# Splitting the last loads of a layer into quarters, in an attention-and-MLP decode kernel on one core

## The chip, the cores and the metric

The kernel runs on one core of one Trainium2 chip. The metric is the device time of one execution in microseconds (us). "Before" is the tuned kernel, "after" is the same kernel with the change. The runs quoted here are of the state "fast".

Names used below: TensorE (PE in the profile, PEld its weight loads), VectorE (DVE), ScalarE (ACT), the sync engine's queue (SPq), which issues all loads, and the 16 DMA engines, which move them.

## The reference, cut to what matters

Two layers of the same thing: attention of one query per batch entry and head over a cached K and V, a projection with `wo`, and an MLP with `w3` and `w4`.

```python
B, Sq, D = 2, 1, 576
H, Sk, Dh = 32, 16384, 128          # K and V: 4 MB each for one (batch, head), bf16
# ...
    q = (x @ wq) ...
    scores = einsum("bhqd,bhkd->bhqk", q, k_cache) * (Dh ** -0.5)
    o = einsum("bhqk,bhkd->bhqd", softmax(scores), v_cache)
    return o... @ wo
# ...
    h2 = gelu(layernorm(x1) @ w3) @ w4
# x -> attention -> MLP -> attention -> MLP, the same weights and caches in both layers
```

There are 64 units (batch x head), each with 8 MB of K and V. They are read in both layers, except for two units that stay on the chip from layer 1 to layer 2. That makes about 1.1 GB of loads with very little arithmetic for each byte.

## The kernel before

One large buffer has three places of 8 MB, each for the K and V of one unit. Weights are laid over parts of the places that are free at the time. `want` queues a load; `pump` issues loads strictly in order, and holds the first one (and with it all behind it) until everything that lies under its destination has been used.

```python
    def pump(self):
        while self.queue:
            keys, p, n, src, sem = self.queue[0]
            under = [t for t in self.live if t["off"] < p + n and p < t["off"] + t["n"]]
            if not all(t["done"] for t in under):
                return
            # ... waits for the readers of what lies under it, then one DMA for each src
```

K and V of a unit come whole (4 MB each), but those of the last unit of a layer, and the first that layer 2 loads, come in halves of 2 MB:

```python
            if split:
                ap = src.rearrange("(t p j) d -> t p (j d)", t=2, p=128)
                for h in range(2):
                    ring.want([(kind, l, u, h)], at + h * self.half, self.half,
                              [lambda e, v, h=h: e.dma_start(v, ap[h])])
            # ...
        for i in range(U - 3, U):                      # the last three V of a layer
            kv("V", l, i, split=i == U - 1)
        want_w34(l, 1, 1 if l == 0 else 2)             # behind them w3 and w4
        if l == 0:
            want_wq(1, 1)                              # and layer 2's wq
```

The second half of the last V lies over the last piece of `wo` (three heads), which is used in the middle of the last unit:

```python
                if i == U - 1 and c == 3:              # last unit, after its fourth chunk
                    self.weigh(l, i - 2, 0)
                    self.weigh(l, i - 2, 1)
                    self.normalize(*mid, self.o[:, slice(*mid)], "o")
                    self.project_pieces(l, [self.n_wo - 1])     # uses wo's last piece
```

So the order at the end of a layer is: all loads up to the first half of the last V are queued some 30 us ahead; then the queue waits for the projection; then come the second half, `w3` and `w4`. `W4_PIECES = (5, 4, 2, 1)` says in how many feature groups `w4` comes; the first piece has a place of its own, the second lies over `w3` in layer 1 and waits until the first two rows of `w3` are used. `weigh` multiplies with a V half only when it has landed:

```python
        vt, res = self.ring.get(self.key("V", l, u, h))
        # ... 64 matmuls with vt
        self.pe(f, r=[*res, f"p{q}"], w=[f"P:ops{q}"])
```

TensorE's instructions of the middle units stand in a loop (two units a turn), those of the other engines are unrolled:

```python
                def run(eng, items=plan[e], loops=self.loops if e == "tensor" else ()):
```

Of the kernel before, what the change touches and what calls it, by code (L numbers as in the profile page):

```python
# [189 lines left out]
class Arena:  # L190
# [34 lines left out]
    def get(self, key):  # L225
        t = self.tiles[key]
        return self.buf[:, t["off"]:t["off"] + t["n"]], t["res"]
# [6 lines left out]
class Decode:  # L234
# [5 lines left out]
    ROT = 12  # L240
    WO_PIECE = 4
    FJ = 3
    W4_PIECES = (5, 4, 2, 1)

    def __init__(self, nc, A_x, K, V, wq, wo, w2, w3, w4, out):
        self.nc = nc
# [91 lines left out]
    def plan(self):  # L338
        ring, B, H, D, KT, U = self.ring, self.B, self.H, self.D, self.KT, self.U
        unit = 2 * self.half  # L340
        self.order = [list(range(U)), list(reversed(range(U)))]
        self.kept = set(self.order[0][-self.N_KEEP:])

        def kv(kind, l, i, split=False):
            u = self.order[l][i]
            if l == 1 and u in self.kept:
                return
            b, hh = u % B, u // B
            src = {"K": self.K, "V": self.V}[kind][b, hh]
            pl = self.place(l, i)  # L350
            at = pl * self.place_n + {"K": 0, "V": unit}[kind]
            if split:
                ap = src.rearrange("(t p j) d -> t p (j d)", t=2, p=128)
                for h in range(2):
                    ring.want([(kind, l, u, h)], at + h * self.half, self.half,
                              [lambda e, v, h=h: e.dma_start(v, ap[h])])
            else:
                ap = src.rearrange("(p j) d -> p (j d)", p=128)
                ring.want([(kind, l, u, h) for h in range(2)], at, unit, [lambda e, v: e.dma_start(v, ap)],
                          sem=f"{kind}{pl}")  # L360

        def rows(kind, l, w, at, last=None):


            n = w.shape[1]
            for k in range(KT):
                if k < KT - 1:
                    ap, m = w[k * 128:(k + 1) * 128, :], n
                else:
                    m = n // 2  # L370
                    ap = w[k * 128:D, :].rearrange("r (c n) -> (r c) n", c=2)
                ring.want([(kind, l, k)], at + k * n if last is None or k < KT - 1 else last, m,
                          [lambda e, v, ap=ap: e.dma_start(v, ap)])  # L373

        def want_wq(l, p):
            rows("wq", l, self.wq, p * self.place_n + unit, last=p * self.place_n + 7 * unit // 8)

        def want_w34(l, p, p1):
            base = p * self.place_n
            rows("w3", l, self.w3, base)  # L380
            at, a0 = base + (2 * KT - 1) * self.F // 2, 0
            for c, n in enumerate(self.W4_PIECES):
                m = n * self.FJ * D
                if c == 1:
                    assert at <= base + self.place_n
                    at = p1 * self.place_n
                ap = self.w4[a0 * 128 * self.FJ:(a0 + n) * 128 * self.FJ, :].rearrange(
                    "(a p j) n -> p a (j n)", p=128, j=self.FJ)
                ring.want([("w4", l, c)], at, m,
                          [lambda e, v, ap=ap, n=n: e.dma_start(v.rearrange("p (a m) -> p a m", a=n), ap)])  # L390
                at, a0 = at + m, a0 + n

        def want_w2(at):
            n = 128 * (KT - 1)
            w2a, w2b = self.w2[0:n, :].rearrange("(p r) n -> p (r n)", p=128), self.w2[n:D, :]
            ring.want([("w2",)], at, KT * D, [lambda e, v: e.dma_start(v[:, 0:(KT - 1) * D], w2a),
                                              lambda e, v: e.dma_start(v[0:64, (KT - 1) * D:KT * D], w2b)])

        def want_wo(l, j, at):
            h0, h1 = self.wo_piece(l, j)  # L400
            ap = self.wo[h0 * 128:h1 * 128, :].rearrange("(j p) n -> p j n", p=128)
            ring.want([("wo", l, j)], at, (h1 - h0) * D,
                      [lambda e, v: e.dma_start(v.rearrange("p (j n) -> p j n", n=D), ap)])

        want_wq(0, 2)
        for l in range(2):
            wp = 2 - 2 * l
            early = 5 if l == 1 else 0
            wo_at = 7 if l == 0 else self.ROT + 1
            gap = max(1, (U - 8 - wo_at) // self.n_wo)  # L410
            for i in range(U):
                kv("K", l, i, split=(l == 1 and i == 2) or i == U - 1)
                if i < early:
                    kv("V", l, i, split=(l == 1 and i == 2))
                elif early <= i - 1 < U - 3:
                    kv("V", l, i - 1)
                j, r = divmod(i - wo_at, gap)
                if r == 0 and 0 <= j < self.n_wo:
                    want_wo(l, j, wp * self.place_n + (2 * unit - self.N_MID * D if j == self.n_wo - 1
                                                            else j * self.WO_PIECE * D))  # L420
                if l == 0 and i == 6:
                    want_w2(wp * self.place_n + unit)
            for i in range(U - 3, U):
                kv("V", l, i, split=i == U - 1)
            want_w34(l, 1, 1 if l == 0 else 2)
            if l == 0:
                want_wq(1, 1)
# [7 lines left out]
        ap = self.wo[h * 128:(h + 1) * 128, :]  # L435
        self.s.dma(lambda e: e.dma_start(self.wolast[:, :], ap), w=["wolast"])

    def key(self, kind, l, u, h):
        return (kind, 0 if u in self.kept else l, u, h)

    def release(self, kind, l, u, h):
        if l == 1 or u not in self.kept:
            self.ring.done(self.key(kind, l, u, h))


    def build(self):
# [215 lines left out]
    def turn(self, l, i, c):  # L662

        u = self.order[l][i]
        h, j0 = divmod(c * self.CH, self.TB)
        kt, res = self.ring.get(self.key("K", l, u, h))
        b, k = c % 3, c % self.NKT

        def f(pe):
            for j in range(self.CH):  # L670
                ins = pe.transpose(self.tps[b][:, j * 128:(j + 1) * 128],  # L671
                                   kt[:, (j0 + j) * 128:(j0 + j + 1) * 128], self.ident[:, :])
            return ins
        self.pe(f, r=[*res, "ident"], w=[f"P:tps{b}"])
        self.act(lambda a: a.activation(out=self.ktsb[k][:, :, :].rearrange("p a b -> p (a b)"), in_=self.tps[b][:, :],  # L675
                                        func=ACT.Copy), r=[f"P:tps{b}"], w=[f"ktsb{k}"])
        self.waiting.append((l, i, c, k))
        if (c + 1) * self.CH == self.TB:
            self.release("K", l, u, 0)
# [13 lines left out]
    def dots(self, l, i, c):  # L693
        u = self.order[l][i]
        h, j0 = divmod(c * self.CH, self.TB)
        kt, res = self.ring.get(self.key("K", l, u, h))
        d = c % 2
        q = i % 2
        k3 = kt.rearrange("p (j d) -> p j d", d=128)[:, j0:j0 + self.CH, :]
        self.dve(lambda v: v.tensor_tensor(out=self.prod[d][:, :, :], in0=k3, in1=bcast_mid(self.qb[q][:, :], self.CH),  # L700
                                           op=ALU.mult), r=[*res, f"qb{q}"], w=[f"prod{d}"])
        o = c * self.CH - self.NCP * self.CH
        self.dve(lambda v: v.tensor_reduce(out=self.sd[q][:, o:o + self.CH], in_=self.prod[d][:, :, :], axis=AX.X,  # L703
                                           op=ALU.add), r=[f"prod{d}"], w=[f"sd{q}"])
        if (c + 1) * self.CH == self.NB:
            self.release("K", l, u, 1)
# [30 lines left out]
    def weigh(self, l, i, h):  # L737
        u = self.order[l][i]
        q = i % 2
        vt, res = self.ring.get(self.key("V", l, u, h))  # L740

        def f(pe):
            for j in range(self.TB):
                ins = pe.matmul(self.ops[q][:, 0:1], lhsT=vt[:, j * 128:(j + 1) * 128],  # L744
                                rhs=self.p[q][:, h * self.TB + j:h * self.TB + j + 1],
                                start=(h == 0 and j == 0), stop=(h == 1 and j == self.TB - 1))
            return ins
        self.pe(f, r=[*res, f"p{q}"], w=[f"P:ops{q}"])
        self.release("V", l, u, h)
        if h == 1 and i < self.U - 1:  # L750
            self.dve(lambda v: v.tensor_copy(out=self.o[:, u:u + 1], in_=self.ops[q][:, 0:1]),
                     r=[f"P:ops{q}"], w=["o"])
# [150 lines left out]
```

## Time and profile before

| | before |
|---|---|
| median of 3 runs | 2578.07 us (2577.87 to 2578.26) |
| loads | 1099.39 MB, mean 427 GB/s |
| DMA busy | 9 tenths or more in 39 of 40 slices |
| busy share of VectorE, TensorE, ScalarE | 77%, 60%, 43% |

The lines of the page of before that bound the kernel: the span; the 40 slices of DMA share and GB/s; and the DMA queues with packets, MB and share of the 16 engines' time.

```profile
span 2575.9 us, 75345 instructions
...
DMA  9999999999999999999999999999999999999998
GB/s 414 431 427 432 431 432 430 432 429 430 433 432 431 431 432 431 432 430 428 406 401 427 428 430 430 430 431 432 431 432 430 430 432 431 431 431 432 429 427 357
...
q1 hardware_dynamic: 51944, 1097.76, 99.6%
q8 instruction: 80, 1.31, 0.2%
q14 instruction: 39, 0.32, 0.0%
```

The loads fill the span. GB/s falls in slices 20 and 21 (end of layer 1, start of layer 2) and in the last one: there, if anywhere, a reordering of loads can gain. The table of stretches of before shows those dips more finely. Its columns: the stretch in us, busy time (and count) of PE, PEld, DVE, ACT, POOL, then the granted TensorE clock, the DMA share and GB/s.

```profile
1266.00:1268.00 2.00, 1.32 (x50) 1.23 (x47) 1.97 (x3) 0.00 (x0) 0.00 (x0) 0.50 0.71 303
1268.00:1270.00 2.00, 0.15 (x5) 0.15 (x6) 1.73 (x4) 0.00 (x0) 0.00 (x0) 0.50 0.68 279
1270.00:1272.00 2.00, 2.00 (x38) 2.00 (x37) 1.51 (x3) 0.67 (x1) 0.00 (x0) 0.50 0.84 229
1272.00:1274.00 2.00, 2.00 (x34) 2.00 (x32) 1.97 (x3) 2.00 (x7) 0.00 (x0) 0.50 0.75 295
...
1294.00:1296.00 2.00, 2.00 (x78) 2.00 (x76) 0.00 (x0) 0.00 (x0) 0.00 (x0) 0.50 0.87 297
1296.00:1298.00 2.00, 1.10 (x40) 1.01 (x37) 0.28 (x2) 0.49 (x2) 0.00 (x0) 0.50 0.85 304
...
2530.00:2532.00 2.00, 1.47 (x55) 1.38 (x52) 1.97 (x3) 0.00 (x0) 0.00 (x0) 0.50 0.82 352
2532.00:2534.00 2.00, 0.00 (x0) 0.00 (x1) 1.88 (x4) 0.00 (x0) 0.00 (x0) 0.50 0.49 197
2534.00:2536.00 2.00, 2.00 (x37) 2.00 (x38) 1.37 (x3) 0.53 (x1) 0.00 (x0) 0.50 0.76 279
2536.00:2538.00 2.00, 2.00 (x33) 2.00 (x32) 1.97 (x3) 2.00 (x7) 0.00 (x0) 0.50 0.93 393
```

Against 430 GB/s the stretches from 1266 to 1274 lose 2.9 us of stream and those from 2530 to 2538 lose 2.3 us (each loses 2 us times what it lacks of 430, over 430). The wait behind the second dip, in the sync queue's own list of waits (line, who ended it, us in total, times, longest):

```profile
SPq L356 <- PE misc L581: 30.2, 1, 30.2
```

Line 356 is the issue of the second half, line 581 is the projection with `wo`. Last, the tail of the chain of waits of before (start, us, what):

```profile
2556.91 15.06 DMA buf<-in_B_w_dram
2571.98 0.05 issue
2572.03 0.57 PE misc L581 x15
```

The kernel ends with a fixed tail of 3.9 us behind the landing of `w4`'s last piece at 2571.98. Whatever is to speed up the end has to bring that landing forward.

The Trainium skill, page "DMA: Bandwidth & Descriptors", section "Why a DMA increments its semaphore by 16 and not by 1", says that the engines of a load finish independently, each adds one to the load's semaphore, and only the full count means that everything has landed. The trace file has the time of every one of these 16 increments (they were read from the file itself; no view of the profile prints them), so it shows not only when a load was complete, but how far apart its fastest and its slowest engine were. They are not told by name; the table gives the first, the 15th and the last. End of layer 2 in before (us from the span's start):

```
load                    issued    first    15th     last
last V, first half      2503.93   2531.04  2539.83  2541.95
last V, second half     2534.59   2541.24  2545.65  2546.85
w3, first rows          2534.96   2543.99  2548.43  2549.63
w4, last piece          2556.91   2566.40  2571.12  2571.98
```

Between the two halves the first increments lie 10.20 us apart, although 2 MB take 4.88 us: the fastest engine stood dry for 5.3 us, that is, it had no load queued. The last ones lie 4.90 us apart: the slowest did not stand at all. This takes it that one and the same engine is last both times. The trace does not name it, but an engine that is done with the first half at 2541.95 and needs 4.88 us for its share of the second cannot be done before 2546.83, and the last increment came at 2546.85.

### The profile page before, as it was taken

How to read it: one execution, taken by the hardware profiler on the slowest of the kernel's cores; microseconds unless marked ns; L12 is line 12 of the kernel's file. 1: busy time of each engine (PE TensorE's matmuls, PEld its weight loads, DVE VectorE, ACT ScalarE, POOL GpSimd, SP SyncE). 2: the span in 40 equal slices, each digit the busy share in tenths (PEclk: the TensorE clock that was granted, in tenths of full speed). 3: DMA queues.
4: the chain of work that ended last, by engine and by line, in shares of the span. 5: the costliest groups of instructions: out<-in, count | busy, mean ns of one | idle time of the engine just before them, and what ended most of it. 6: DMA issues, size and time to landing. Idle time of an engine off the chain costs nothing.

```text
span 2575.9 us, 75345 instructions
## 1 busy us (share of the span) xinstructions
PE 1546.1 (60%) x34519; PEld 1459.3 (57%) x34519; DVE 1977.9 (77%) x2781; ACT 1111.2 (43%) x1809; POOL 0.8 (0%) x10
## 2 busy tenths in 40 slices
PE   5655555655556555656667765556555555566666
PEld 5555555555555555555657765555555555555555
DVE  5877787778777777878759987777787777778875
ACT  3444444444444444444435544444444444444442
POOL 0000000000000000000000000000000000000000
PEclk8666666666666666666655666666666666666665
DMA  9999999999999999999999999999999999999998
GB/s 414 431 427 432 431 432 430 432 429 430 433 432 431 431 432 431 432 430 428 406 401 427 428 430 430 430 431 432 431 432 430 430 432 431 431 431 432 429 427 357
DMA packets 52063, 1099.39 MB, mean 427 GB/s; under 512 B 4900, under 2 KB 13160, under 8 KB 16872
## 3 DMA queue, kind: packets, MB, share of 16 engines
q1 hardware_dynamic: 51944, 1097.76, 99.6%
q8 instruction: 80, 1.31, 0.2%
q14 instruction: 39, 0.32, 0.0%
HBM read 1097.74 MB, written 0.00 MB: 426 GB/s over the span
## 4 chain that ended last, share of the span: by engine, by line
DMA 54%; DVE 38%; PE 6%; SPq 1%; issue 1%; ACT 0%; DVEq 0%
DMA buf<-in_A_k_cache_dram 52%; DVE sd L703 24%; DVE prod L700 13%; PE tps L671 4%; DMA buf<-in_B_w_dram 2%; PE misc L721 2%; DVE small L723 1%; SPq L390 1%; DMA buf<-in_A_wq_dram 1%; SPq L373 0%; PE misc L581 0%; DVE small L715 0%; DVE small L713 0%; DVE small L711 0%; PE misc L493 0%
## 5 line engine op out<-in xcount | busy, mean ns | idle before, releaser
L675 ACT ACTIVATE ktsb<-tps 128x1024 bf16<-128x1024 bf16 x1024 | 1004.7, 1028 | 886.2 <-PE tps L671 880.8
L703 DVE TENSOR_REDUCE sd<-prod 128x8 f32<-128x1024 bf16 x1024 | 1249.3, 1220 | 35.5
L671 PE MATMUL tps<-ident,buf 128*128 128x128 bf16 x8192 | 839.3, 270 | 642.8 <-DMA buf<-in_A_k_cache_dram 639.5
L671 PEld LDWEIGHTS tps<-ident,buf 128*128 128x128 bf16 x8192 | 681.1, 124 | 671.2 <-DMA buf<-in_A_k_cache_dram 659.9
L700 DVE TENSOR_TENSOR prod<-buf,qb 128x1024 bf16<-128x1024 bf16 x1024 | 697.7, 681 | 11.2 <-DMA buf<-in_A_k_cache_dram 10.3
L744 PE MATMUL ops<-p,buf 128*128 128x1 bf16 x16384 | 466.7, 165 | 181.2 <-DMA buf<-in_A_v_cache_dram 169.9
L744 PEld LDWEIGHTS ops<-p,buf 128*128 128x128 bf16 x16384 | 448.7, 102 | 191.7 <-DMA buf<-in_A_v_cache_dram 179.5
L688 PE MATMUL sps<-qcur,ktsb 128*128 128x1 bf16 x8192 | 352.5, 166 | 94.1 <-ACT ktsb L675 85.5
L723 DVE TENSOR_REDUCE small<-misc 128x1 f32<-128x128 f32 x128 | 37.4, 292 | 467.0 <-PE misc L721 467.0
L688 PEld LDWEIGHTS sps<-qcur,ktsb 128*128 128x128 bf16 x8192 | 318.0, 103 | 131.7 <-ACT ktsb L675 129.3
L659 ACT ACTIVATE qb<-misc 128x128 bf16<-128x128 f32 x128 | 35.5, 277 | 489.2 <-PE misc L656 489.2
L721 PE MATMUL misc<-identS,small 128*128 128x128 f32 x256 | 95.7, 477 | 51.1 <-DVE small L715 39.4
L721 PEld LDWEIGHTS misc<-identS,small 128*128 128x128 f32 x256 | 69.5, 332 | 55.0 <-DVE small L715 41.7
L732 ACT ACTIVATE p<-sd,small 128x64 bf16<-128x64 f32 x128 | 45.3, 354 | 0.0
L732 ACT ACTIVATE p<-sps,small 128x64 bf16<-128x64 f32 x128 | 40.5, 316 | 11.0 <-DVE small L723 11.0
L651 ACT ACTIVATE qcur<-qt 128x1 bf16<-128x1 bf16 x128 | 29.0, 226 | 19.4 <-DVE qt L588 19.4
L656 PE MATMUL misc<-ident,qcur 128*128 128x128 bf16 x128 | 34.1, 267 | 1.1 <-ACT qcur L651 1.1
L711 DVE TENSOR_REDUCE small<-sps 128x1 f32<-128x64 f32 x128 | 27.4, 214 | 0.0
L732 ACT ACTIVATION_READ_ACCUMULATOR p<-sps,small 128x1 f32 x128 | 27.0, 211 | 0.0
L713 DVE TENSOR_REDUCE small<-sd 128x1 f32<-128x64 f32 x128 | 26.6, 208 | 0.0
L732 ACT ACTIVATION_READ_ACCUMULATOR p<-sd,small 128x1 f32 x128 | 26.4, 206 | 0.0
L545 PE MATMUL sps<-xn,buf 128*128 128x2 bf16 x544 | 16.7, 166 | 14.0 <-DMA buf<-in_A_wq_dram 9.5
(75 smaller groups left out, 163.4 us busy)
## 6 DMA issues: line engine op xcount, KB each, us to landing
buf<-in_A_k_cache_dram SPq DMA_DIRECT2D x123, 4096.0 KB, 22.5
buf<-in_A_v_cache_dram SPq DMA_DIRECT2D x123, 4096.0 KB, 31.9
buf<-in_A_k_cache_dram SPq DMA_DIRECT2D x6, 2048.0 KB, 27.0
buf<-in_A_v_cache_dram SPq DMA_DIRECT2D x6, 2048.0 KB, 16.3
buf<-in_B_w_dram SPq DMA_DIRECT2D x8, 1152.0 KB, 18.1
buf<-in_A_wq_dram SPq DMA_DIRECT2D x8, 1024.0 KB, 10.0
buf<-in_A_wo_dram SPq DMA_DIRECT2D x14, 576.0 KB, 32.8
buf<-in_B_w_dram SPq DMA_DIRECT2D x2, 2160.0 KB, 27.1
```

The lines of the kernel that those rows point to most:

```text
L651: self.act(lambda a: a.activation(out=self.qcur[:, q:q + 1], in_=self.qt[:, u:u + 1], func=ACT.Copy), r=["qt"], w=[f"qcur{q}"])
L656: self.pe(lambda pe: pe.matmul(self.misc[:, 0:128], lhsT=bcast(self.qcur[:, q:q + 1], 128), rhs=self.ident[:, :], start=True, stop=True), ...
L659: self.act(lambda a: a.activation(out=self.qb[q][:, :], in_=self.misc[:, 0:128], func=ACT.Copy), r=["P:misc"], w=[f"qb{q}"])
L671: ins = pe.transpose(self.tps[b][:, j * 128:(j + 1) * 128], kt[:, (j0 + j) * 128:(j0 + j + 1) * 128], self.ident[:, :])
L675: self.act(lambda a: a.activation(out=self.ktsb[k][:, :, :].rearrange("p a b -> p (a b)"), in_=self.tps[b][:, :], func=ACT.Copy), r=[f"P:t ...
L688: ins = pe.matmul(self.sps[sp][:, col:col + 1], lhsT=self.ktsb[k][:, j, :], rhs=self.qcur[:, sp:sp + 1], start=True, stop=True)
L700: self.dve(lambda v: v.tensor_tensor(out=self.prod[d][:, :, :], in0=k3, in1=bcast_mid(self.qb[q][:, :], self.CH), op=ALU.mult), r=[*res, f ...
L703: self.dve(lambda v: v.tensor_reduce(out=self.sd[q][:, o:o + self.CH], in_=self.prod[d][:, :, :], axis=AX.X, op=ALU.add), r=[f"prod{d}"], ...
L721: self.pe(lambda pe: pe.matmul(self.misc[:, 128:256], lhsT=bcast(self.m[:, q:q + 1], 128), rhs=self.identS[:, :], start=True, stop=True), ...
L723: self.dve(lambda v: v.tensor_reduce(out=self.bias[:, q:q + 1], in_=self.misc[:, 128:256], axis=AX.X, op=ALU.max, negate=True), r=["P:misc ...
L732: self.act(lambda a, c0=c0, c1=c1, src=src, part=part: a.activation(out=self.p[q][:, c0:c1], in_=src, func=ACT.Exp, bias=self.bias[:, q:q ...
L744: ins = pe.matmul(self.ops[q][:, 0:1], lhsT=vt[:, j * 128:(j + 1) * 128], rhs=self.p[q][:, h * self.TB + j:h * self.TB + j + 1], start=(h ...
```

## The change

Read from the code, the intent is this. Only the upper part of the last V's second half lies over `wo`. If the half comes as two quarters, the lower one need not wait, and 1 MB more is queued over the wait. The same holds for the second half of layer 2's first loaded K, whose upper quarter alone lies over `wq`'s last piece (K and V share the code, so all six split tensors get the quarters: six more DMAs). With `w4` in pieces of 6, 3, 2 and 1, 432 KB more are queued before the wait for `w3`. The products still wait for both quarters.

```diff
-    W4_PIECES = (5, 4, 2, 1)
+    W4_PIECES = (6, 3, 2, 1)
 ...
-                for h in range(2):
-                    ring.want([(kind, l, u, h)], at + h * self.half, self.half,
-                              [lambda e, v, h=h: e.dma_start(v, ap[h])])
+                quarter = self.half // 2
+                ring.want([(kind, l, u, 0)], at, self.half, [lambda e, v: e.dma_start(v, ap[0])])
+                for k in range(2):
+                    ring.want([(kind, l, u, 1 + k)], at + (2 + k) * quarter, quarter,
+                              [lambda e, v, k=k: e.dma_start(v, ap[1][:, k * quarter:(k + 1) * quarter])])
 ... (get and release then name one half or its two quarters)
```

More of the change, by code (lines that the diff above doesn't have):

```diff
@@ L436, in load_wo_last, with halves, get @@
         self.s.dma(lambda e: e.dma_start(self.wolast[:, :], ap), w=["wolast"])
-    def key(self, kind, l, u, h):
-        return (kind, 0 if u in self.kept else l, u, h)
+    def halves(self, kind, l, u, h):
+        l = 0 if u in self.kept else l
+        keys = [(kind, l, u, h), (kind, l, u, 2)]
+        return keys if h == 1 and keys[1] in self.ring.tiles else keys[:1]
+    def get(self, kind, l, u, h):
+        found = [self.ring.get(k) for k in self.halves(kind, l, u, h)]
+        off = self.ring.tiles[self.halves(kind, l, u, h)[0]]["off"]
+        return self.buf[:, off:off + self.half], [r for _, res in found for r in res]
     def release(self, kind, l, u, h):
         if l == 1 or u not in self.kept:
-            self.ring.done(self.key(kind, l, u, h))
+            for k in self.halves(kind, l, u, h):
+                self.ring.done(k)
     def build(self):
@@ L665, in turn @@
         h, j0 = divmod(c * self.CH, self.TB)
-        kt, res = self.ring.get(self.key("K", l, u, h))
+        kt, res = self.get("K", l, u, h)
         b, k = c % 3, c % self.NKT
@@ L695, in dots @@
         h, j0 = divmod(c * self.CH, self.TB)
-        kt, res = self.ring.get(self.key("K", l, u, h))
+        kt, res = self.get("K", l, u, h)
         d = c % 2
@@ L739, in weigh @@
         q = i % 2
-        vt, res = self.ring.get(self.key("V", l, u, h))
+        vt, res = self.get("V", l, u, h)
         def f(pe):
```

## The prediction

> **What bounds the kernel now.** The page: DMA is at 9 tenths in 39 of 40 slices, 427 GB/s over a span of 2575.9 us; DVE is busy 77%, PE 60%. It is DMA-bound; a change without fewer bytes can only remove holes in the DMA stream or shorten the tail. The table of stretches shows four holes (against some 430 GB/s):
> - 1266-1274 us, end of layer 1: 303, 279, 229, 295 GB/s, 2.9 us lost. In the queue's waits, the last V's second half waits 30.7 us for the PE (wo's last heads lie in its upper part), until 1270.4.
> - 1295-1297 us: 1 us lost, w4's second piece waits 20.7 us for w3's use.
> - 1320-1324 us: 262, 213, 311, 328 GB/s, 1.4 us; K's second half waits 11.6 us for wq's last piece.
> - 2530-2536 us, end of layer 2: 352, 197, 279, 2.3 us; the same wait as the first (30.2 us).
>
> **What the change does.** No byte and no matmul goes. A quarter (1 MB, 2.4 us of the stream at 9.7 us per 4 MB) of each last V can be issued 30 us earlier, as can one of layer 2's first K. w4's first piece grows by 432 KB (1.05 us), so more is queued before the wait at 1295. Six DMAs are added; the matmuls still wait for both quarters. From the mean rate this would give 1 to 2 us at the end of layer 1, 1 at the start of layer 2, 2 at the end: 3 to 5 us.
>
> **Why I expect almost none of it.** A load's semaphore gets 16 increments. The Trainium skill, "DMA: Bandwidth & Descriptors", section "Why a DMA increments its semaphore by 16 and not by 1", says that the engines finish independently and only the full 16 means that all has landed. The trace agrees: near 1250 us the first and last increments of one load lie 10.8 us apart, near 2510 us 10.0. The last increment keeps its pace through every hole. First hole: last V's halves at 1277.77 and 1282.66 (4.89 us; elsewhere 4.88), then w3 at 2.79 each, w4 5.22, 4.22. At the end: 2541.95, 2546.85, on to w4's last piece at 2571.98. The slowest engine is never dry; others are, and the spread falls from 10.8 to 5.4 us. Only layer 2's first K, second half, takes 5.83; 0.95 us extra also comes about every 120 us without any wait, so I take it for something else. The chain of waits ends at w4's last landing, with 3.9 us of fixed tail. Filling the other engines' holes doesn't move it. Cost: a split load takes 4.88+4.88 instead of 9.71, so by estimate 0.03 us per extra DMA, 0.2 in all.
>
> **Predicted: 2577.8 us**, 8 in 10 within 2576.0 to 2579.0. Faster by over 2%: 0.005; within 2%: 0.99; slower: 0.005.
>
> **What would show it.** Right: the holes at 1266, 1320 and 2530 shrink in the table of stretches, the one at 1295 deepens to about 2.5 us, w4's last landing stays at 2571-2572. Wrong: it comes 2 to 4 us earlier.
>
> **What would make it wrong.** The last increments might not always be the same engine's; then filled holes help. If the engines share one limit, the slowest might have run faster while others idled. A shift of the 0.95 us events could move the end by 1 us.

## The result, and the profile after

| | median | range | runs |
|---|---|---|---|
| before | 2578.05 us | 2577.80 to 2578.26 | 6 |
| after | 2578.47 us | 2577.89 to 2579.33 | 6 |

The ratio of after to before is 1.0002, 95% interval 0.9989 to 1.0015: the same. That interval reaches from 2.8 us faster to 3.9 us slower; the ranges of the runs are much narrower.

The table of stretches of after, the same stretches as shown of before:

```profile
1266.00:1268.00 2.00, 1.55 (x59) 1.47 (x56) 1.97 (x4) 0.00 (x0) 0.00 (x0) 0.50 0.97 410
1268.00:1270.00 2.00, 0.00 (x0) 0.00 (x0) 1.93 (x4) 0.00 (x0) 0.00 (x0) 0.50 0.84 344
1270.00:1272.00 2.00, 1.91 (x36) 1.91 (x37) 1.31 (x4) 0.43 (x1) 0.00 (x0) 0.50 0.77 287
1272.00:1274.00 2.00, 2.00 (x34) 2.00 (x33) 1.97 (x3) 2.00 (x6) 0.00 (x0) 0.50 0.94 389
...
1294.00:1296.00 2.00, 2.00 (x81) 2.00 (x79) 0.00 (x0) 0.00 (x0) 0.00 (x0) 0.50 0.70 212
1296.00:1298.00 2.00, 0.78 (x30) 0.69 (x27) 0.56 (x3) 0.49 (x2) 0.00 (x0) 0.50 0.93 342
...
2530.00:2532.00 2.00, 2.00 (x81) 2.00 (x79) 1.97 (x3) 0.00 (x0) 0.00 (x0) 0.50 1.05 438
2532.00:2534.00 2.00, 0.23 (x9) 0.14 (x6) 1.97 (x3) 0.00 (x0) 0.00 (x0) 0.50 0.97 406
2534.00:2536.00 2.00, 1.24 (x24) 1.24 (x25) 1.31 (x5) 0.00 (x0) 0.00 (x0) 0.50 0.59 246
2536.00:2538.00 2.00, 2.00 (x33) 2.00 (x32) 1.94 (x3) 1.77 (x6) 0.00 (x0) 0.50 0.94 332
```

So the change did what it was meant to do to the mean rate: by the same sum the dip at 1266 to 1274 went from 2.9 to 1.3 us, that at 2530 to 2538 from 2.3 to 1.4 us (0.3 us more lies just ahead of it, at 2528 to 2530). The wait itself is as long as before (it now belongs to the upper quarter), and the landing that the tail hangs on did not come earlier. The list of waits and the tail of the chain of after:

```profile
SPq L358 <- PE misc L592: 29.5, 1, 29.5
```

```profile
2558.06 14.76 DMA buf<-in_B_w_dram
2572.82 0.05 issue
2572.86 0.57 PE misc L592 x15
```

The increments at the end of layer 2 in after, read as before:

```
load                    issued    first    15th     last
last V, first half      2504.88   2531.83  2540.28  2542.80
   lower quarter        2505.36   2534.29  2542.74  2545.27
   upper quarter        2535.35   2539.91  2545.22  2547.76
w3, first rows          2535.72   2542.72  2548.01  2550.53
w4, last piece          2558.06   2565.06  2571.87  2572.82
```

The first increment gained: from the first half to `w3` it now takes 10.89 us (2542.72 less 2531.83), before it took 12.95. The last one takes 7.73 us, before it took 7.68. The engines that had stood dry were given something to do; the one that everything waits for had not been dry, and is no sooner done.

### The profile page after: what moved, and what is told of

Its sections match the earlier page's. It is cut to its first block, busy times and chain, and to the rows that moved or that the text cites. A ratio compares the mean times of both kernels' runs of the same rounds, so it can differ in the third digit from the quotient of the medians.

```text
span 2576.7 us, 75357 instructions
## 1 busy us (share of the span) xinstructions
PE 1546.0 (60%) x34519; PEld 1457.5 (57%) x34519; DVE 1978.0 (77%) x2781; ACT 1111.4 (43%) x1809; POOL 0.8 (0%) x10
## 4 chain that ended last, share of the span: by engine, by line
DMA 54%; DVE 38%; PE 6%; SPq 1%; issue 1%; ACT 0%; DVEq 0%
DMA buf<-in_A_k_cache_dram 52%; DVE sd L714 24%; DVE prod L711 13%; PE tps L682 4%; DMA buf<-in_B_w_dram 2%; PE misc L732 2%; SPq L392 1%; DVE small L734 1%; DMA buf<-in_A_wq_dram 0%; SPq L375 0%; PE misc L592 0%; DVE small L726 0%; DVE small L724 0%; DVE small L722 0%; PE misc L504 0%
```

## The experiments

The theory, "slowest engine": a load counts as landed when its slowest DMA engine is done, and that engine does not run dry in these dips, so filling them is worth nothing. The first rival, "mean rate": a dip in GB/s costs its depth, and something in the change ate the gain. The second, "holes never matter": something other than the loads bounds the ends of the layers, so that no hole there matters. Twelve kernels were run, all in five timed rounds. Each group was run beside before on one chip; before's medians there were 2577.87 us (e1 to e4), 2577.81 (e5 to e8), 2577.96 (e9, e10) and 2577.76 (e11, e12). By 95% intervals e5, e6, e7, e8 and e12 are faster and e9 is slower; for the others the interval holds 1, also for e3 (0.9995 to 1.0022), whose range nevertheless lies wholly above before's.

| run | edit | median (range), us | ratio to before |
|---|---|---|---|
| e1 | quarters only | 2578.06 (2577.94 to 2578.68) | 1.0001 |
| e2 | `w4` pieces only | 2577.74 (2577.53 to 2578.29) | 1.0000 |
| e3 | last V whole | 2580.00 (2579.10 to 2580.58) | 1.0009 |
| e4 | three quarters early | 2578.46 (2578.14 to 2578.54) | 1.0002 |
| e5 | 1 MB less before the hole | 2573.26 (2572.40 to 2574.03) | 0.9982 |
| e6 | 1 MB less after the hole | 2572.60 (2572.31 to 2572.89) | 0.9980 |
| e7 | VectorE in the loop | 2571.88 (2571.70 to 2572.03) | 0.9977 |
| e8 | VectorE in the loop, on after | 2572.60 (2572.34 to 2573.40) | 0.9981 |
| e9 | late release, on before | 2586.46 (2585.27 to 2587.01) | 1.0033 |
| e10 | late release, on after | 2579.63 (2579.17 to 2580.29) | 1.0007 |
| e11 | control of e7 | 2576.90 (2576.55 to 2577.60) | 0.9997 |
| e12 | VectorE and ScalarE in the loop | 2572.29 (2571.66 to 2572.72) | 0.9978 |

### e1 and e2: the two parts of the change alone

e1 is after with `W4_PIECES` set back to (5, 4, 2, 1); e2 is before with (6, 3, 2, 1).

> The quarters alone, w4's pieces as before (5, 4, 2, 1). Theory 'slowest engine' (the last of a load's 16 increments never runs dry, so only its bytes count): within 0.5 us of before, last piece of w4 landing at 2571.5 to 2573, first hole filled in the table of stretches, the hole at 1295 deeper than in after, because less is queued before it. Rival 'mean rate' (holes in the stream cost their depth): at least 2 us faster at the end of layer 2, where nothing stands in the way. Rival 'two effects cancel' (quarters gain, w4's new pieces lose): 1 to 3 us faster than before.

> w4 in pieces of 6, 3, 2, 1 alone, the halves as before. 'Slowest engine': within 0.5 us of before. 'Mean rate': 1 us faster (432 KB more before the wait at 1295). 'Two effects cancel': 1 to 3 us slower than before.

Neither part moves the time: e1 is 0.2 us above before, e2 0.1 us below, both within the ranges. So the zero of the sum is not a gain and a loss that cancel. As expected, the hole at 1292 to 1298 is deeper in e1 than in after (2.4 us against 1.6 by the same sum), and it costs nothing either. In the profile of e1 the last piece of `w4` landed at 2572.20 us, in that of e2 at 2572.64, in that of before at 2571.98.

### e3 and e4: less and more queued over the wait

```diff
e3, on before:
-                kv("V", l, i, split=i == U - 1)
+                kv("V", l, i)
e4, on after, for the last V only:
-   quarters at half / 2
+   cut = 3 * self.half // 4        # 1.5 MB early, 0.5 MB waits
```

> The opposite of the change: the last V of each layer comes as one load of 4 MB, all of which waits for wo's last heads, so 2 MB (4.9 us of stream) less are queued before the wait. 'Slowest engine': in before its last landing ahead of the hole is 1277.77 of the V half; without that half it is 1272.87, so its data end about 1 us before the late load arrives; it loses about 1 us at each end of a layer: 2579 to 2581. 'Mean rate': the hole deepens by up to 4.9 us at each of two places, 2583 to 2588.

> After, but three quarters of the last V's second half come early and one quarter waits for wo: 0.5 MB more is queued over the wait. 'Slowest engine': within 0.5 us of after (2578.5), the spread of increments around the hole up by about 1 us from 8.3, the hole at 2534 nearly gone. 'Mean rate': another 1 us faster than after, at the end of layer 2.

With 2 MB less over the wait (e3) the loss is 2.1 us for both layers together, where the mean rate asks for 5 to 10. With 0.5 MB more than in after (e4) nothing comes, although the dip at 2530 to 2538 shrinks further, from 1.4 to 0.9 us (it was expected to be nearly gone). The reserve that this shows can be worked out from the traces. In e9, below, the engines are all dry when layer 1's late half is issued, and its first increment comes 7.05 us later; 4.88 of these are 2 MB at full pace, so 2.17 us pass on the way. (The same sum gives 1.8 to 2.0 us for engines that stood dry in before and in e3, so the reserves below may be up to 0.4 us larger.) In before, the last increment of the first half came at 1277.77 in layer 1, the late half was issued at 1270.45: the slowest engine had 1277.77 - 1270.45 - 2.17 = 5.15 us to spare. In e3 the last one before the late load came at 1272.70, the issue at 1270.26: 0.27 us to spare. So e3 sits at the edge, and the 1 us per layer that it does lose is more than the 0 that this sum gives. Its traces show where it goes: of the 16 increments of the whole V, 14 lie within 0.9 us in layer 1 and within 0.6 us in layer 2, and two come 0.9 us or more behind these. Two 16 KB instruction packets of queue 8 lie in each of the two stretches (at 1275.73 and 1282.04 us, and at 2541.14 and 2547.06 us); that they set two engines back is argued, not shown.

### e5 and e6: bytes before a hole count like bytes after it

```diff
on before (h == 0 in e5, h == 1 in e6):
+                    n = self.half // 2 if kind == "V" and i == U - 1 and h == 0 else self.half
-                              [lambda e, v, h=h: e.dma_start(v, ap[h])])
+                              [lambda e, v, h=h, n=n: e.dma_start(v[:, 0:n], ap[h][:, 0:n])])
```

Both kernels read old data where nothing was loaded. (The comparison with the reference passed all the same: a quarter of one V of 64 is below its tolerance, so it says nothing here.)

> Wrong result on purpose: of the last V's first half only 1 MB is loaded, in both layers, so 1 MB (2.43 us of stream) less comes before the hole. 'Mean rate': the queue runs dry 2.4 us sooner and waits as long as before for the wo heads, so the time stays (within 0.5 us of before). 'Slowest engine': it is never dry, so bytes before a hole count like any: its landings move up by 2.4 us in each layer, in layer 1 as far as layer 2's start lets it through; at least 2.0 us faster than before from the end of layer 2 alone, up to 4.9.

> Wrong result on purpose: of the last V's second half, which waits for the wo heads, only 1 MB is loaded, in both layers, so 1 MB less comes after the hole. Both theories: 2.0 to 4.9 us faster than before. 'Slowest engine': as much as with 1 MB less before the hole, within 0.6 us. 'Mean rate': at least 2 us more than that.

This is the sharpest test of the mean rate. A queue that runs dry and then waits for something else gains nothing from less work ahead of the wait. e5 gains 4.5 us from 1 MB less ahead of it in each layer, e6 gains 5.2 us from 1 MB less behind it (0.7 apart, where within 0.6 was expected); 1 MB in each layer is 4.9 us of stream. In layer 1, the last increment of the second half moved from 1282.66 us to 1280.14 in e5 and to 1280.35 in e6. The bytes ahead of the hole are on the critical path, although most engines wait in it: in before, fifteen of the 16 increments, each taken by its place in the order of time, lose 1.2 to 5.6 us in layer 1's hole and only the last keeps its pace. (In layer 2 the first seven lose 1.8 to 5.6 us, and the other nine keep theirs to within 1 us.)

### e9 and e10: the same change, where the slowest engine does run dry

```diff
on before (e9) and on after (e10):
-                if i == U - 1 and c == 3:
+                if i == U - 1 and c == 7:
```

> The kernel before, but the last unit projects with the wo heads that lie under the last V after its eighth chunk instead of its fourth, so V's second half is let go about 7.4 us later (4 more chunks of 1.85 us on VectorE). In before the slowest engine's data of the first half end about 4 us after the late half arrives; so now it must run dry. 'Slowest engine': about 3 us lost at each end of a layer, 2582 to 2586. 'Holes never matter' (something else bounds the ends of the layers): within 1 us of before.

> The same late release in the kernel after. 'Slowest engine': here the quarter that comes early lies over a wait in which the slowest engine is dry, so it must pay, up to 2.4 us at each end of a layer: 3 to 5 us faster than the late release in the kernel before, 2578.5 to 2581. If quarters never pay, whoever is dry: the same as the late release in the kernel before.

The projection that lets the late load go comes 7.5 us later in layer 1 (1277.96 instead of 1270.45 us), which is more than the 5.15 us to spare. e9 loses 8.5 us, slightly more than the 4 to 8 expected. On the same kernel, the change now gains 6.8 us: 2579.63 against 2586.46. The rival "holes never matter" falls here: holes matter as soon as the last engine is in them, and quarters fill them. (The rival "mean rate" expects this gain too; it fell in e1, e4 and e5.) The increments at the end of layer 2:

```
e9                      issued    first    15th     last
last V, first half      2509.52   2535.65  2543.99  2546.79
last V, second half     2546.79   2553.69  2554.44  2555.62
w3, first rows          2547.16   2556.47  2557.22  2558.42

e10                     issued    first    15th     last
   lower quarter        2505.76   2535.33  2544.91  2545.07
   upper quarter        2542.56   2546.96  2547.92  2547.99
w3, first rows          2542.93   2549.76  2550.78  2551.36
```

In e9 the last increments of the halves lie 8.83 us apart, for data worth 4.88: now the slowest engine too was dry, for 3.9 us. In e10 the quarters lie 2.92 apart, for 2.44. The table of stretches, first of e9, then of e10, shows that this hole looks different from the one in before; it goes down to almost nothing:

```profile
2540.00:2542.00 2.00, 0.15 (x6) 0.06 (x3) 1.97 (x3) 0.00 (x0) 0.00 (x0) 0.50 0.55 221
2542.00:2544.00 2.00, 0.00 (x0) 0.00 (x0) 1.97 (x4) 0.00 (x0) 0.00 (x0) 0.50 0.16 66
2544.00:2546.00 2.00, 0.00 (x0) 0.00 (x0) 1.93 (x5) 0.00 (x0) 0.00 (x0) 0.50 0.09 33
```

```profile
2538.00:2540.00 2.00, 0.00 (x0) 0.00 (x0) 1.97 (x3) 0.00 (x0) 0.00 (x0) 0.50 0.59 254
2540.00:2542.00 2.00, 0.03 (x1) 0.03 (x2) 1.85 (x4) 0.00 (x0) 0.00 (x0) 0.50 0.55 225
2542.00:2544.00 2.00, 2.00 (x76) 2.00 (x77) 0.17 (x1) 0.00 (x0) 0.00 (x0) 0.50 0.62 188
```

The gain was expected at 3 to 5 us and is 6.8. Counted up to `w3`'s first rows, the end of layer 1 gave 2.3 us (1289.41 against 1287.07) and the end of layer 2 another 2.9 (what 2558.42 against 2551.36, 7.1 us, adds to the 4.2 by which e10 was ahead at the first half). Between the two, in the middle of layer 2, another 1.9 us arose: in the profile of e10 two instruction packets (at 1935 and 2055 us, see e7) did not set the last increment back, while in e9 each of their counterparts cost it 1 us. That is one profile each, and chance may be in it.

### e7, e8, e11, e12: what makes one engine the slowest

In before, the last increment keeps the pace of 9.71 us for 4 MB, but for 0.95 to 1.0 us extra at intervals of about 120 us; thereby its lag behind the first grows from 2.0 us at the start to 10 us near the end of layer 1. The page labels some packets of queue 14 "instruction". The skill's page "DMA: Bandwidth & Descriptors", section "Queues, rings and completion order", says that row 14 is internal to the runtime and names the refill among its uses; the page "Runtime: NRT & Kernel Launch", section "Instruction fetch mechanics", says that each sequencer fetches its instructions by its own DMA queue, 256 instructions to 16 KiB. The trace agrees that instruction packets come on queue 14, 39 of them (80 more, of 16 KB, come on queue 8); those of queue 14 are 8 KB, which by that page's figures would be 128 instructions (an estimate). VectorE runs 2781 instructions in 128 units of some 20 us, so 128 of them last about 120 us (an estimate). The packets of queue 14 that fall in step with the losses, with the load whose last increment lost:

```
packet at   took    load landed   last increment lost
412.03      0.33    413.52        1.02
532.27      0.33    542.20        0.97
657.40      0.33    661.28        0.95
778.05      0.33    780.70        0.96
898.28      0.33    899.77        0.98
1019.37     0.32    1028.10       0.96
1138.11     0.33    1145.62       0.98
```

Two more, at 291.76 and 1250.19 us, do the same. The other packets of queue 14 in this stretch, some 180 us apart, leave the last increment alone; behind four of them (618.97, 800.33, 978.65 and 1163.78 us) it is the 15th increment that loses 0.7 us. This fits packets that fall on different engines; the trace does not name the engines.

If these are VectorE's instructions, a loop takes them away. VectorE's work differs between units in one copy only (`o`), which e7 moves to ScalarE; e11 does that move alone.

```diff
e7 on before, e8 on after:
-  loops=self.loops if e == "tensor" else ()
+  loops=self.loops if e in ("tensor", "vector") else ()
e7, e8, e11:
-            self.dve(lambda v: v.tensor_copy(out=self.o[:, u:u + 1], in_=self.ops[q][:, 0:1]),
+            self.act(lambda a: a.activation(out=self.o[:, u:u + 1], in_=self.ops[q][:, 0:1], func=ACT.Copy),
```

> VectorE's instructions in the loop that the TensorE has (the copy of o, the only one that differs between units, goes to ScalarE). About 2050 of 2781 fewer VectorE instructions to fetch. The slowest engine loses 0.97 us every 120 us beside an instruction packet of queue 14, and 128 instructions of VectorE last about 120 us: if these fetches are what makes one engine the slowest, the spread at the end of layer 1 falls from 10 to about 5 us, at the end of layer 2 from 10.9 to 8 or less, and the kernel gets 1 to 3 us faster (the 15th increment lies 1.8 us before the last at layer 2's start and 0.9 us at the end). If the lag has another cause, spread and time stay.

> The same loop on the kernel after. 'Slowest engine': once the slowest engine is less behind, it runs dry in the holes too (the 15th increment lost 2.5 us in the first hole, 1.0 us at the end), so now the quarters pay: 0.5 to 2 us faster than the loop on the kernel before. 'Holes never matter': the same time as the loop on the kernel before.

> Control of the vector loop: only the copy of o goes from VectorE to ScalarE, VectorE's instructions stay unrolled. If the loop's 5.9 us came from fewer instruction fetches, this is within 1 us of before and the last increments still lag by about 10 us at the end of layer 1; if they came from the moved copy, it is about 5 us faster.

> The vector loop on the kernel before, and ScalarE's instructions in the same loop too. With VectorE's fetches gone the slowest engine still loses 0.65 to 0.85 us every 175 us, at the pace of 128 ScalarE instructions. If these are ScalarE's fetches, those losses go (about 5 in layer 1 and 5 in layer 2) and the kernel gets 1 to 4 us faster than the vector loop alone (2571.9); if not, it stays at 2571.9.

e7 is 5.9 us faster than before, the best kernel; the move of the copy alone (e11) gives about 0.9 of these (its range and before's just touch). The page of e7 has fewer fetches on queue 14, and the chain's last landing is 5.8 us earlier:

```profile
q14 instruction: 25, 0.20, 0.0%
```

```profile
2551.23 15.00 DMA buf<-in_B_w_dram
2566.22 0.05 issue
2566.27 0.57 PE misc L581 x15
```

The losses of 0.97 us every 120 us are gone from the last increment; its lag at the end of layer 1 is 6.6 instead of 10.8 us (last V, first half), and 10.1 instead of 10.9 at the end of layer 2, where 5 and 8 were expected. The gain is larger than the 1 to 3 us expected. That expectation compared the last increment with the 15th after the hole. But the whole end of layer 1 moves with the last landing of the last but one K: 1242.79 us in before, 1238.00 in e7.

That also explains why the expectation for e8 failed: with the loop, the quarters do not gain, they cost 0.7 us (2572.60 against 2571.88). The wait for `wo` is itself started by a landing. In before, the projection comes 27.66 us after the last landing of the last but one K (1242.79 to 1270.45), and from that landing to that of the last V's first half the slowest engine has 34.98 us of work. In e7 the same two stretches are 27.46 and 35.59 us. At the end of layer 2 they are 27.65 and 35.01 us in before, 27.46 and 35.60 in e7. So in both traces the reserve of the slowest engine is 5 to 6 us (the second stretch less the first, less 2.17), however far that engine lags. The halves of the kernel before suffice for it, and quarters add nothing until the release comes later than that, as it does in e9.

In e7 the last increment still loses 0.65 to 0.85 us every 160 to 175 us. With ScalarE in the loop too (e12, units addressed by the loop's counter) these losses are gone: from 155 to 1100 us the last increment loses nothing, and the page counts 15 packets on queue 14. But the time stays at 2572.29, so the 1 to 4 us that were expected in this case did not come. By 1238 us the last landing of the last but one K is where it was (1238.03 against 1238.00): near the layers' ends, where TensorE's instructions are unrolled, 80 packets of 16 KB come on queue 8, and single engines lose about 1.3 to 1.5 us there. They now make the slowest engine. That these packets are TensorE's is argued from where they stand, not shown.

## Why the prediction was right, point by point

- **The time**: 2578.47 us measured, 2577.8 predicted, within the range, and the same within 2%. The sign of the small difference was wrong: 0.3 us faster was written down, 0.4 us slower was measured. Both are about the spread of the runs. e1 and e8 also lie above their partners (0.2 and 0.7 us), so a small cost of the change is likely. The prediction's estimate of 0.03 us for each of six DMAs is neither confirmed nor refuted by this; its own numbers (4.88 + 4.88 against 9.71) give 0.05, so 0.3 us in all.
- **The bound**: right. e5 and e6 show that 1 MB anywhere near these waits is worth its 2.4 us.
- **The holes shrink in the table of stretches**: right for those at 1266 (2.9 to 1.3 us), at 2530 (2.3 to 1.4 us), and at 1320 us. The one at 1295 deepens, but from 1.2 to 1.4 us and not to 2.5: the engines do not run dry together, and a sum that treats them as one stream is too large.
- **The slowest engine is never dry, so filling is worth nothing**: right. e1, e4, e5 and e6 agree with it, and e9 with e10 shows the other side: there it is dry, and there the same change gains 6.8 us. That the last increments are always one engine's, which the prediction named as a risk, is inferred from their even pace; the trace names no engine.
- **The engines share one limit**: named as a way to be wrong, and excluded by before itself: with others idle, the last increment needed 4.90 us for 2 MB, elsewhere 4.88.
- **Layer 2's first K, 5.83 us for a half, is not a hole**: right. In e3 the same half was issued with as little to spare (4.18 us before the landing ahead of it, in before 4.16) and took 4.90 us.
- **w4's last landing stays at 2571 to 2572**: missed by 0.8 us: 2572.82 in the profile of after, so a little late, and not the 2 to 4 us early that would have refuted the prediction.
- **What was not foreseen**: that the reserve is built in. The prediction took it as a fact of this trace that the slowest engine was ahead of the wait. e7 and e8 show that it hardly changes when that engine is faster: it is set by how much is queued ahead of the wait and by when the wait ends.

## What to carry to other kernels

A dip in the mean bandwidth is not yet a loss: ask of each load when its first and its last engine were done, and whether the last one was ever without work. If it was not, more loads queued over the wait bought nothing here, and what helped was fewer bytes, or taking away what makes one engine the last: here VectorE's unrolled instructions, whose loop gave some 5 us (5.9 with the moved copy) where the filled holes gave none. Before splitting a load further, work out the reserve (landing ahead, minus issue, minus the time on the way), and split only if it is near zero or below: e3, with 0.27 us to spare, already lost 1 us per layer.

## What the Trainium skill lacked or had wrong

- "Runtime: NRT & Kernel Launch", section "Instruction fetch mechanics", calls the cost of crossing a block "mostly hidden", and says that kernels prefer full unrolling. For the engine that fetches, nothing here contradicts this; for a kernel bound by loads it is not so. One 8 KB packet that took 0.33 us set the last increment of a load back by 0.97 us, and VectorE in a loop instead of unrolled made the kernel 5.9 us faster (0.9 of it from a copy moved).
- The same section gives refills of 16 KiB. On queue 14 the trace has 8 KB packets, on queue 8 it has 16 KB.
- "DMA: Bandwidth & Descriptors" tells that only the full count of 16 means landed, but not how far apart the engines drift in a long stream: 2.0 us on the first K, 10 us after 1200 us. Beyond a remark on the pace of bulk loads, no page says what follows for a dip in mean GB/s, that it costs nothing while the last engine is busy (2.3 us of dip at the end of layer 2, no gain when it shrank).
- The same page has a fit of 2.0 us fixed cost for each DMA for the path issued from GpSimd. It gives no such fit for loads issued from the sync engine. To idle DMA engines, 2.17 us passed beyond the time of the data in e9, and 1.8 to 2.0 us in before and e3.
